# A hand-written order for the first batch: a new order of pieces, other engines for some of them, and exponentials over two PSUM banks

## The chip, the cores and the metric

The kernel runs on one core of a Trainium2 chip. The metric is the time of one execution in device microseconds (us), the median of several runs. The profile is one further execution, taken apart by engine: PE (TensorE, matmuls and transposes), ACT (ScalarE), DVE (VectorE), POOL (GpSimd), SP (SyncE, which here only starts DMAs).

## The reference

Attention over heads with normed queries and keys, then an MLP with a residual, for 8 batches of 448 tokens, 12 heads of 64:

```python
q_n, k_n = rmsnorm(q, g_q), rmsnorm(k, g_k)               # over the last axis, 64
scores = q_n @ k_n.T / 8 ; attn = softmax(scores)
x = (attn @ v), heads side by side                        # 8 x 448 x 768
xn = (x - mean) / sqrt(var + 1e-6) * g_ln
out = x + relu(xn @ w_ch1) @ w_ch2                        # 768 -> 3072 -> 768
```

## The kernel before

Heads are worked in pairs: pair p is heads 2p and 2p+1 of a batch, so pairs 0 to 5 are batch 0 and 6 to 11 batch 1. Pairs come in units that are loaded and normed together: units 0 and 1 are pairs 0 and 1, unit 2 is pairs 2 and 3, unit 3 pairs 4 and 5, and from unit 4 on each unit is two pairs. The matmuls take fp16 operands; a key is split into a high and a low fp16 part.

From batch 1's MLP on, loops set the order of the work. All that comes before that, batch 0 and the attention of batch 1 up to pair 12, is written out by hand as one list of short names, `ORDER`. `first_attention` walks the list and calls one closure for each name. Every engine takes its instructions strictly in the order of that list, and waits where an operand or a buffer isn't ready. `ENGINE` says for some names which engine does them (A is ACT, V is DVE, P is POOL); the rest have a usual engine.

The names that the text uses:

- keys of unit u in batch 0: `a` square, `d` sum, `h` root (`h0` to `h3`, `hq`, `hr`; each is two short ACT instructions), `n` scale, `j` high part, `k` low part; then for pair p `Kp` is the transposition on PE and `Cp` the copy out of PSUM. Later units add `b`, `c`, `e`, `g`, `i`, `l`, `m` (queries, root, weights) and `Qp`, `Dp`.
- queries of batch 0, by phase and first pair (`q0.2`): `qa` square, `qt` sum, `qG` times the weight, `ql` scale, `qm` doubling, `Q` transposition, `QC` copy out of PSUM. `sp1`, `spm`, `sp2` make the product of the two norm weights (a small PE matmul in between).
- `Sph.p.k`, `Eph.p.k`, `Vph.p`: scores, exponential and values of phase ph (a third of the query rows) of pair p in batch 0. A phase 0 or 1 score takes two banks, k = 0 (512 columns) and k = 1 (384). `O`, `T`, `A`, `N`, `X`, `XC`: the attention's output, its layer norm, and the transposition of the normed tokens.
- `Ut.k`: 24 matmuls of the first MLP layer for token tile t and 512 of the 3072 columns of w_ch1, `Rt.k` the relu that empties its bank. `Ht.g.k`, `Jt.g`, `Pt.g`: second layer, residual, store.
- `L5k`: load of unit 5's keys. `W0`, `W1`, `W2`: thirds of w_ch1 (1024 columns each), started by POOL; `U?.0` and `U?.1` need W0, `U?.2` and `U?.3` W1, `U?.4` and `U?.5` W2. `W3.k`, `W4.k`: quarters of the halves of w_ch2. `B0`, `B2`...: a tiny POOL copy that waits for a load, and so holds back the W behind it (`BEHIND` says which load).
- `F12`: 12 filler matmuls, whose result nobody reads.

PSUM has eight banks: one for transpositions (`tr`), two for scores (pool `ps_s`, tile `psS`), two for values (`ps_o`, tiles `oA` and `oB`) and three for the MLP, the query transpositions and a few others (`ps_m`). So a 512-column score sits in one bank, and each exponential reads one bank.

## Time and profile before

| | |
|---|---|
| time, median of 3 runs | 591.55 us (591.08 to 592.36) |
| profiled execution | 591.01 us, of which the span from first to last instruction 589.4 us |
| PE busy | 577.6 us (98%) |
| ACT, DVE, POOL busy | 353.0, 291.7, 189.5 us |
| granted TensorE clock | 1.00 throughout |
| end of the listed part (last `H`) | about 111 us after the start |

A busy PE is one with a matmul in flight; the ends of matmuls are modelled. The DMA share is the mean busy share of 16 DMA engines, where more than 1.00 means that transfers overlap on an engine. A row of the timeline is: start, length, engine, line, operation, tiles, shapes, count, and in brackets the idle time just before with what ended it.

### The profile page before, as it was taken

Reading aid. Unit: us, or ns where it says so; the run is one execution under the profiler, and the core shown is the slowest. Engines: PE = TensorE matmul, PEld = TensorE weight load, DVE = VectorE, ACT = ScalarE, POOL = GpSimd, SP = SyncE. Lnnn points to the kernel's source line nnn. Section 1 sums busy time; section 2 is a strip of 40 time slices with the busy share of each in tenths; the row PEclk is TensorE's granted clock in tenths of the full one; section 3 lists DMA queues with packets and bytes.
Section 4 is the critical chain, followed back from the end, with each engine's and each line's share of the span. In section 5 each row is a group of like instructions: output and inputs, shape, how many; then the busy total and the mean of one; then the engine's idle time right before and its main releaser. Section 6 shows DMA issues by size and latency. Waiting matters only on the chain.

```text
span 589.4 us, 12424 instructions
## 1 busy us (share of the span) xinstructions
PE 577.6 (98%) x4971; PEld 360.4 (61%) x4971; DVE 291.7 (49%) x636; ACT 353.0 (60%) x666; POOL 189.5 (32%) x258
## 2 busy tenths in 40 slices
PE   5899999999999999999999999999999999999997
PEld 5799976545666666545566666655566566654565
DVE  6999688345545456624446256815266222540011
ACT  5999773488752997178842797358844477124300
POOL 4648261065350665044350465342502000000000
PEclk9999999999999999999999999999999999999999
DMA  8999998573594987843779596844823220030011
GB/s 266 226 246 219 228 220 213 115 192 89 114 181 125 132 161 115 191 131 66 124 133 158 99 140 140 174 133 92 155 59 88 69 63 1 33 103 1 1 53 57
DMA packets 130321, 75.25 MB, mean 128 GB/s; under 512 B 96564, under 2 KB 120452, under 8 KB 130260
## 3 DMA queue, kind: packets, MB, share of 16 engines
q1 hardware_dynamic: 113712, 44.94, 37.3%
q0 software_dynamic: 16224, 29.27, 23.7%
q8 instruction: 40, 0.66, 0.5%
q10 hardware_dynamic: 324, 0.21, 0.1%
q14 instruction: 21, 0.17, 0.1%
HBM read 52.30 MB, written 11.01 MB: 107 GB/s over the span
## 4 chain that ended last, share of the span: by engine, by line
PE 95%; SPq 2%; DVE 1%; DMA 1%; ACT 0%; issue 0%
PE psC L1090 37%; PE psH L1056 33%; PE psS L408 8%; PE oA L477 5%; PE psU L749 4%; PE oB L479 2%; PE psS L426 2%; PE psS L693 1%; SPq L167 1%; SPq L175 1%; PE oA L725 1%; DMA qkv<-in_q_dram 1%; PE tr L345 1%; PE tr L362 0%; ACT E L704 0%; DVE khl L573 0%
## 5 line engine op out<-in xcount | busy, mean ns | idle before, releaser
L1090 PE MATMUL psC<-w,hT 128*128 128x384 f16 (+1 forms) x1368 | 235.6, 323 | 0.0
L1056 PE MATMUL psH<-xnT,w 128*128 128x512 f16 (+1 forms) x1008 | 217.3, 356 | 0.0
L440 ACT ACTIVATE E<-psS,rr_all 128x448 f16<-128x448 f32 x264 | 164.6, 636 | 58.3 <-PE psS L408 57.6
L1090 PEld LDWEIGHTS <-hT 128*128 128x128 f16 x1368 | 128.2, 98 | 75.9 <-issue 0.4
L1058 ACT ACTIVATE hT<-psH 128x512 f16<-128x512 f32 (+1 forms) x168 | 93.7, 558 | 112.3 <-PE psH L1056 110.8
L1056 PEld LDWEIGHTS <-w 128*128 128x128 f16 x1008 | 91.1, 98 | 77.0 <-issue 2.1
L408 PE MATMUL psS<-qU,kU 128*128 128x448 f16 x252 | 86.3, 352 | 0.0
L477 PEld LDWEIGHTS <-E 128*128 128x128 f16 x792 | 53.6, 98 | 34.4 <-issue 2.1
L1097 DVE SCALAR_TENSOR_TENSOR x<-psC,rs_all,x 128x384 f32<-128x384 f32 x48 | 29.0, 616 | 75.6 <-PE psC L1090 75.1
L274 POOL TENSOR_TENSOR qkv<-qkv,gprod 128x896 f32<-128x896 f32 x19 | 39.5, 2079 | 76.9 <-ACT khl L116 62.4
L477 PE MATMUL oA<-v,E 128*128 128x65 f16 x756 | 57.8, 193 | 0.1
L490 DVE RECIPROCAL rec_all<-oA 128x6 f32<-128x6 f32 x42 | 8.2, 195 | 88.6 <-PE oA L477 88.2
L167 POOL DMA_DIRECT2D qkv<-in_k_dram x14 | 11.1, 796 | 118.3 <-ACT E L440 53.4
L266 DVE TENSOR_REDUCE ssq<-khl 128x14 f32<-128x896 f32 x21 | 22.7, 1083 | 53.3 <-ACT khl L116 53.2
L479 PE MATMUL oB<-v,E 128*128 128x65 f16 x252 | 45.0, 193 | 0.1
L408 PEld LDWEIGHTS <-kU 128*128 128x128 f16 x252 | 24.3, 98 | 15.3
L266 DVE TENSOR_REDUCE ssq<-qn 128x14 f32<-128x896 f32 x21 | 22.8, 1084 | 21.1 <-ACT qn L116 21.1
L91 DVE SCALAR_TENSOR_TENSOR qn<-qkv,rr_all 128x256 f16<-128x256 f32 (+2 forms) x71 | 25.3, 416 | 15.1 <-ACT rr_all L270 15.1
L749 PE MATMUL psU<-xnT,w 128*128 128x128 f16 x432 | 27.0, 219 | 0.0
L749 PEld LDWEIGHTS <-w 128*128 128x128 f16 x432 | 25.2, 98 | 1.5 <-issue 0.4
L479 PEld LDWEIGHTS <-E 128*128 128x128 f16 x264 | 25.4, 96 | 0.3 <-DVE xl L497 0.2
L492 DVE TENSOR_TENSOR x<-oA,rec_all 128x384 f32<-128x384 f32 x42 | 23.4, 558 | 1.3
(161 smaller groups left out, 602.5 us busy)
## 6 DMA issues: line engine op xcount, KB each, us to landing
out_dram<-x SPq DMA_DIRECT2D x20, 384.0 KB, 2.6
qkv<-in_v_dram POOLq DMA_DIRECT2D x15, 384.0 KB, 6.6
qkv<-in_k_dram POOLq DMA_DIRECT2D x14, 384.0 KB, 4.0
qkv<-in_q_dram POOLq DMA_DIRECT2D x14, 384.0 KB, 4.9
w<-in_moe_w_ch_dram POOLq DMA_DIRECT2D x3, 1536.0 KB, 13.2
...
```

The costliest lines, as they stand in the source:

```text
L91: nc.vector.scalar_tensor_tensor(out=out, in0=x, scalar=8.0, in1=r.unsqueeze(2).broadcast_to([x.shape[0], g, D]), op0=ALU.mult, op1=ALU.mult)
L266: nc.vector.tensor_reduce(out=c["ssq"][:, n], in_=c["sq", n], axis=AX.X, op=ALU.add)
L274: _on(nc, f"i{u}", "P").tensor_tensor(out=self.loads[u][1], in0=self.loads[u][1], in1=sh.gprod.unsqueeze(1).broadcast_to([128, g, D]), op= ...
L408: self.nc.tensor.matmul(ps[:, 0:S], c["main"][:, ts(i, 128)], c["q"][:, ts(i // 3, S)], start=True, stop=True)
L440: self.nc.scalar.activation(out=o, in_=c.pop(("ps", i))[:, 0:S], func=AFT.Exp, scale=self.units[u][3][:, g:g + 1], bias=EXP_BIAS)
L477: nc.tensor.matmul(oA[:, t, cs], E[:, ts(t, 128)], rhs, start=(i == 0 and t == 0), stop=(i == 6 and t == 2))
L479: nc.tensor.matmul(oB[:, cs], E[:, 320:448], rhs, start=(i == 0), stop=(i == 6))
L749: nc.tensor.matmul(ps[:, ts(f, 128)], sh.w1[:, dc, ts(4 * k + f, 128)], self.xnT[:, dc, ts(t, 128)], start=(f == 0 and dc == 0), stop=(f = ...
L1056: nc.tensor.matmul(ps[:, 0:N], sh.w1[:, dc, ts(f, 128)], xnT[:, dc, 0:N], start=(dc == 0), stop=(dc == NDC - 1))
L1058: nc.scalar.activation(out=hT[:, f, 0:N], in_=ps[:, 0:N], func=AFT.Relu)
L1090: nc.tensor.matmul(self.psC[:, 0:g[1]], self.hT[:, f, ts(t, 128)], sh.w2[:, h, f, c:c + g[1]], start=(f == 0), stop=(f == NFF - 1))
L1097: self.nc.vector.scalar_tensor_tensor(out=x, in0=self.sums.pop((b, t, g[0]))[:, 0:g[1]], scalar=self.rs[:, b, t:t + 1], in1=x, op0=ALU.mul ...
```

## The change

1. `ORDER` is a new list. It holds the same pieces, but for twelve exponentials that are merged into twelve others, two new pieces `I9` and `I10` (a one-column POOL memset that claims the buffer of unit 9 or 10 ahead of its load), and the fillers: 91 matmuls before, 143 after.
2. `ENGINE` gives other engines to some 45 pieces. Of those ahead of the first `U`: `n0 n1 k0 k1 ql0.2 qa2.4 qG2.0` go to POOL; `j0 j3 qG0.0 qG0.2 QC0.0 qm2.0 qm2.4` to DVE; `C0 C3 QC1.0 QC2.2 QC2.4` to ACT. Later: seven of the relus from ACT to DVE, and squares, casts and subtractions of units 4 to 8 mostly to POOL.
3. The two halves of a phase 0 or 1 score lie in one tile of two banks, read by one exponential of 896 columns. There are two such tiles (pools `ps_w0`, `ps_w2`). After the twelfth they are closed and their four banks become single banks; two of them go to scores, two join bank 4 for the MLP. Until then bank 4 alone serves all that `ps_m` served.
4. The keys' fp16 parts of batch 0 get room of their own in `hT`, and the key transpositions alternate between two banks (`tr` and the bank of `oB`).
5. `W0` waits for the last values of batch 0 (`BEHIND[0]`) instead of the keys of unit 4; `W1` no longer follows at once.

```diff
-BEHIND = {0: (4, 1), 2: (5, 2), 3: (6, 2), 4: (7, 2)}
+BEHIND = {0: (0, 2), 2: (5, 1), 3: (6, 1), 4: (7, 1)}
 ORDER = """
-F12 a0 a1 d0 h0 sp1 spm qa0.0 n0 sp2 qt0.0 d1 qG0.0 j0 h1 k0 L4k G ql0.0 n1 F14 K0 Q0.0 j1 L4q a2
+a0 d0 h0 a1 L4k F12 n0 qa0.0 j0 F8 sp1 qt0.0 F14 d1 k0 F10 spm F5 h1 sp2 K0 qG0.0 a2 n1 F4 F2 j1
+ql0.0 F4 F9 d2 k1 G Q0.0 L4q QC0.0 C0 qa0.2 qa1.0 F39 qt0.2 F5 h2 K1 qG0.2 ql0.2 B0 n2 F6 W0 a3
...
-        self.ps_s = pool("ps_s", 2, space=PSUM)
-        self.ps_m = pool("ps_m", 3, space=PSUM)
+        self.room = {4: pool("ps_4", 1, space=PSUM)}
+        for at in (0, 2):
+            self.whole[at] = tc.tile_pool(name=f"ps_w{at}", bufs=1, space=PSUM, side=SIDE[at])
+            self.room[at] = self.whole[at].__enter__()
+        self.n_wide, self.wide, self.idle, self.free, self.read, self.free_s = 0, [2, 0], [4], [], {}, False
+        self.tr2 = self.ps_o.tile([128, 1024], FP16, tag="oB", name="tr2")
+    def two_banks(self):
+        at = self.wide.pop(0)
+        self.n_wide += 1
+        if self.n_wide == 2 * NPAIR:
+            for x in self.wide:
+                self.wide_read(x)
+        return at, self.room[at].tile([128, 1024], FP32, tag=f"wide{at}", name="psW")
+    def wide_read(self, at):
+        if self.n_wide < 2 * NPAIR:
+            self.wide.append(at)
+            return
+        self.whole[at].__exit__(None, None, None)
+        for y in (at, at + 1):
+            self.room[y] = self.ctx.enter_context(
+                self.tc.tile_pool(name=f"ps_{y}", bufs=1, space=PSUM, side=SIDE[at]))
+        if not self.free_s:
+            self.free_s = True
+            self.free += [at + 1, at]
+        else:
+            self.idle += [at, at + 1]
+    def score_psum(self):
+        at = self.free.pop(0)
...
+    def mlp_psum(self):
+        self.at = self.idle.pop(0)
+        return self.bank(self.at)
...
         def power(ph, p, k):
-            width = 192 if ph == 2 else 128
+            if ph < 2:
+                nc.scalar.activation(out=E[ph, p], in_=psS[ph, p][:, 0:896], func=AFT.Exp,
+                                     scale=0.125, bias=EXP_BIAS)
+                self.wide_read(psS["at", ph, p])
+                return
...
+                ops[f"C{p}"] = lambda p=p: self.moved(f"C{p}", kT[p], banks[p % 2][:, 0:960])
...
-                warm["ps"] = self.ps_o.tile([128, 3, 130], FP32, tag="oB", name="psW")
+                warm["ps"] = self.ps_o.tile([128, 3, 130], FP32, tag="oA", name="psW")
...
+            ops[f"I{u}"] = lambda u=u: nc.gpsimd.memset(self.load_tile(u)[1][:, 0, 0:1], 0.0)
```

Three places of the new order follow, each as instructions of one engine. DVE from the sum of unit 0's key squares (`d0`) on, before; `hT` is the buffer that holds the keys, `khl` their fp16 parts, `L566` is `n0` and `n1`, `L573` is `k0` and `k1`:

```order
L555 TENSOR_REDUCE ssq<-khl 128x7
L795 TENSOR_TENSOR gprod<-w_62 1x64
L566 TENSOR_TENSOR hT<-hT,rr_all 128x448
L800 COPY gprod<-psG 128x64
L555 TENSOR_REDUCE ssq<-qn 128x4
L555 TENSOR_REDUCE ssq<-khl 128x7
L573 TENSOR_TENSOR khl<-hT,khl 128x7x64
L612 TENSOR_TENSOR qn<-qkv,rr_all 128x4x64
L566 TENSOR_TENSOR hT<-hT,rr_all 128x448
L785 COPY kT<-tr 128x960
L573 TENSOR_TENSOR khl<-hT,khl 128x7x64
```

The same stretch of DVE after (`five` is a single bank):

```order
L627 TENSOR_REDUCE ssq<-hT 128x7
L117 CAST hT<-hT 128x7x64
L889 TENSOR_TENSOR gprod<-w_62 1x64
L627 TENSOR_REDUCE ssq<-qn 128x4
L627 TENSOR_REDUCE ssq<-hT 128x7
L894 COPY gprod<-five 128x64
L679 TENSOR_TENSOR qkv<-qkv,gprod 128x4x64
L686 TENSOR_TENSOR qn<-qkv,rr_all 128x4x64
L627 TENSOR_REDUCE ssq<-hT 128x14
L879 COPY qU_100<-five 128x512
```

The scaling, the low parts and the copy of pair 0's keys have left DVE; a cast (`j0`), a weighting (`qG0.0`) and the copy of the first queries (`QC0.0`) have come, and the copy of `gprod`, which waits for the small PE matmul, stands behind both sums.

ACT at the first exponentials, before; each reads one bank `psS`:

```order
L783 COPY qU_106<-psQ 128x1024
L704 ACTIVATE E<-psS 128x512
L704 ACTIVATE E<-psS 128x384
L601 ACTIVATE qn<-qkv 128x4x128
L601 ACTIVATE qn<-qkv 128x4x64
L704 ACTIVATE E<-psS 128x512
L601 ACTIVATE qn<-qkv 128x2x128
L601 ACTIVATE qn<-qkv 128x2x64
L704 ACTIVATE E<-psS 128x384
L704 ACTIVATE E<-psS 128x512
```

And after, where `psW` is a tile of two banks:

```order
L599 ACTIVATE rt<-ssq 128x26
L600 ACTIVATE rr_all<-rt 128x26
L782 ACTIVATE E<-psW 128x896 x2
L877 COPY kT<-tr_126 128x960
L123 ACTIVATE khl<-qkv 128x4x128
L123 ACTIVATE khl<-qkv 128x4x64
L877 COPY qU_101<-five 128x768
L782 ACTIVATE E<-psW 128x896 x2
L599 ACTIVATE rt<-ssq 128x12
```

Two exponentials have become one, the second root `h3` stands ahead of all of them, and two copies that DVE made are between them.

POOL around the loads of w_ch1 (`L963`), before: W0 and W1 stand together, behind the poke that waits for unit 4's keys, and ahead of the values' casts (`L661`, `L666`):

```order
L605 TENSOR_TENSOR qkv<-qkv,gprod 128x12x64
L838 COPY poke<-w_62 128x2
L963 DMA w_68<-in_moe_w_ch_dram 128x6x1024 x2
L661 CAST v_108<-qkv 128x12x64 x2
L666 CAST vl<-qkv 64x2x64 x4
L661 CAST v_108<-qkv 128x12x64
L666 CAST vl<-qkv 64x2x64 x2
L887 TENSOR_SCALAR gln<-gln 128x768
```

After, from W0 to W1 (W2 follows three instructions later):

```order
L1060 DMA w_68<-in_moe_w_ch_dram 128x6x1024
L679 TENSOR_TENSOR qkv<-qkv,gprod 128x12x64
L742 CAST vl<-qkv 64x2x64
L737 CAST v_102<-qkv 128x12x64 x2
L742 CAST vl<-qkv 64x2x64 x3
L125 TENSOR_TENSOR khl<-qkv 128x2x128
L125 TENSOR_TENSOR khl<-qkv 128x2x64
L742 CAST vl<-qkv 64x2x64 x2
L737 CAST v_102<-qkv 128x12x64
L679 TENSOR_TENSOR qkv<-qkv,gprod 128x8x64
L679 TENSOR_TENSOR qkv<-qkv,gprod 128x256
L1060 DMA w_68<-in_moe_w_ch_dram 128x6x1024
```

W0 is now ahead of the query weighting, and W1 behind all the values' casts.

200 lines of the change are left out of this document (125 added, 75 removed).

## The prediction

> **What bounds the kernel now.** I read the page first, then the engines by stage, then PE's timeline. The engines' busy times and the chain that ended last:
>
> ```profile
> PE 577.6 (98%) x4971; PEld 360.4 (61%) x4971; DVE 291.7 (49%) x636; ACT 353.0 (60%) x666; POOL 189.5 (32%) x258
> PE 95%; SPq 2%; DVE 1%; DMA 1%; ACT 0%; issue 0%
> ```
>
> PE sets the end. The change keeps every matmul but the fillers, so it can only win where PE waits, or lose by new waits. By stages of 10 us (busy us of each engine, clock, DMA share, GB/s):
>
> ```profile
> 10.00:20.00 10.00, 8.69 (x130) 7.37 (x127) 9.94 (x13) 9.23 (x17) 3.84 (x5) 1.00 1.04 289
> 20.00:30.00 10.00, 9.36 (x166) 7.94 (x163) 9.93 (x19) 9.37 (x24) 9.61 (x14) 1.00 1.08 224
> 30.00:40.00 10.00, 9.94 (x182) 9.59 (x180) 9.86 (x20) 9.55 (x23) 5.87 (x6) 1.00 1.12 220
> 40.00:50.00 10.00, 10.00 (x190) 9.59 (x187) 8.90 (x18) 8.74 (x17) 6.55 (x9) 1.00 1.02 256
> 50.00:60.00 10.00, 10.00 (x172) 9.17 (x170) 9.74 (x17) 9.77 (x19) 6.87 (x10) 1.00 1.18 223
> ```
>
> From 10 to 30 us DVE is full (9.94 and 9.93 of 10), ACT nearly so, and PE waits; from 30 us on PE is full. DMA is full throughout. PE's timeline at the start, at its last idle row, and at the first `U`:
>
> ```profile
> 3.75 1.46 PE L879 MATMUL psW<-id 128*128 128x128 f16 x12 [3.75 <-POOL id masks.py:199]
> 9.31 0.29 PE L342 MATMUL tr<-id,khl 128*128 128x128 f16 x1 [1.50 <-DVE khl L573]
> 13.93 2.34 PE L879 MATMUL psW<-id 128*128 128x128 f16 x39
> 27.98 0.65 PE L693 MATMUL psS<-qU,kT 128*128 128x128 f16 x6 [0.22 <-ACT E L704]
> 34.76 1.50 PE L749 MATMUL psU<-xnT,w 128*128 128x128 f16 x24
> ```
>
> After 27.98 no wait is left, and from the first `U` (34.76) MLP blocks fill every gap. In both lists the PE pieces ahead of the first `U` are the same (one third of a score is exchanged for another), so the arrival of the first `U`, called T here, measures the start: 34.76 before. What follows is T's shift, then whether PE still runs without waits behind it.
>
> **DVE up to T.** Prices per instruction (mean ns after the count's busy us):
>
> ```profile
> L566 DVE TENSOR_TENSOR hT<-hT,rr_all 128x448 f32<-128x448 f32 x2 | 1.2, 622 | 1.6 <-ACT rr_all L540 1.6
> L573 DVE TENSOR_TENSOR khl<-hT,khl 128x448 f16<-128x448 f32 x2 | 1.2, 622 | 0.0
> L785 DVE COPY kT<-tr 128x960 f16<-128x960 f16 x3 | 2.0, 655 | 0.0
> L785 DVE COPY qU<-psQ 128x768 f16<-128x768 f16 x5 | 2.8, 552 | 0.0
> L605 DVE TENSOR_TENSOR qkv<-qkv,gprod 128x512 f32<-128x512 f32 x1 | 0.7, 683 | 0.0
> L605 DVE TENSOR_TENSOR qkv<-qkv,gprod 128x256 f32<-128x256 f32 x1 | 0.5, 517 | 0.0
> ```
>
> Gone: `n0 n1 k0 k1` 4 x 0.622 = 2.49; `ql0.2`, 512 wide, 0.68; `C0 C3` 2 x 0.655 = 1.31; `QC1.0 QC2.2` 2 x 0.552 = 1.10; `qG2.0` 0.683 + 0.517 = 1.20; together 6.8. Come: `qG0.0` 0.52 and `qG0.2` 0.68. `j0`, `j3`, `QC0.0`, `qm2.0` and `qm2.4` have no row on DVE: at most the two-operand price of their widths or that of the copy (0.62 + 1.24 + 0.55 + 0.55 + 0.55 = 3.5), at least about 1.5, if a copy between fp16 tiles (0.39 for 896, quoted below) sets the scale. I take 2.0, nearer to the copies, because four of the five have one operand of fp16 or PSUM. Net: 6.8 - 1.2 - 2.0 = 3.6 us less on the engine that is full; 2.1 to 4.1 by the ends.
>
> Not all of it shortens T, since the chain now hops between engines. `n0` and `k0` go to POOL, which has room: it waited 4.3 and 4.6 us in this stage.
>
> ```profile
> POOL poke L838 <- DMA w<-in_k_dram: 4.6, 1, 4.6
> POOL qkv L605 <- DVE gprod L800: 4.3, 1, 4.3
> L605 POOL TENSOR_TENSOR qkv<-qkv,gprod 128x512 f32<-128x512 f32 x1 | 1.3, 1268 | 0.9 <-ACT qn L601 0.9
> L274 POOL TENSOR_TENSOR qkv<-qkv,gprod 128x896 f32<-128x896 f32 x3 | 6.2, 2080 | 0.1
> ```
>
> At 448 of 512 each POOL instruction takes about 1.1, half a microsecond longer than on DVE; but `h0` no longer stands behind `a1`, whose data came late, which gives about a microsecond back. So `K0` comes at about 8.5 to 9.6 against 9.31. POOL's own sum up to T grows by about 4.5 (`n0 n1 k0 k1`) + 1.3 (`ql0.2`) + 1.2 (`qa2.4`) + 2.0 (`qG2.0`), less 3.3 for what it gives away: 5.7, inside its waits.
>
> New waits on DVE: the `gprod` copy now stands behind a PE matmul that has 44 fillers ahead of it. The first twelve took 1.46, 0.12 each, so 44 end at 3.75 + 5.4 = 9.1 if PE stays so slow, at about 7.5 if it speeds up to the 0.06 of the row at 13.93. DVE reaches the copy at about 8.3, so it waits 0 to 1.4; I take 0.7, and everything queued on DVE behind it waits too, `ql0.0` and `d2` first. `n3` waits for the root `h3`, which stands on ACT behind the 1024-wide copy `QC0.2`: 0.6 of idle, 0 to 1. Together 1.3. The 52 added fillers cost nothing else, because PE waits for the keys' chain there; without that cover they are 52 x 0.06 = 3.1.
>
> ACT's sum up to T hardly moves by the exchanged pieces. The exponentials:
>
> ```profile
> L704 ACT ACTIVATE E<-psS 128x512 f16<-128x512 f32 x16 | 9.5, 597 | 0.7 <-PE psS L693 0.2
> L704 ACT ACTIVATE E<-psS 128x384 f16<-128x384 f32 x15 | 7.4, 490 | 0.4 <-PE psS L697 0.3
> L783 ACT COPY kT<-tr 128x960 f16<-128x960 f16 x1 | 0.9, 942 | 0.0
> ```
>
> Two took 1.09; one of 896 takes 0.92 if each 128 columns cost 0.107 as between the rows, 0.94 by the 960-wide copy, and 1.09 if crossing a bank costs something. Twelve times that is 0 to 2.0 less. I leave 0 in the sum: DVE, not ACT, carries the layer norm ahead of T. One bank instead of three for the query transpositions makes each `Q` wait for the copy before it; those stand a copy's length apart in the list, so 0, at most one copy, 0.94.
>
> **POOL and DVE at once.** These two can block each other here. Counts, then one DVE copy and the POOL instruction beside it:
>
> ```profile
> L319 DVE COPY qn<-qn x19: 382/394/1749, 40.5 to 467.0; 128x896 f16<-128x896 f16 x19
> 68.22 1.75 DVE L319 COPY qn<-qn 128x896 f16<-128x896 f16 x1
> 67.64 2.08 POOL L274 TENSOR_TENSOR qkv<-qkv,gprod 128x896 f32<-128x896 f32 x1
> ```
>
> The copy that usually takes 0.39 took 1.75, and ended just after the POOL instruction (69.97 against 69.72). The change puts 9 us more work on POOL ahead of T and gives DVE four such copies or casts (`j0`, `j3`, `qm2.0`, `qm2.4`). `j0` is safe, POOL waits for it. The other three can lose up to 1.36 each, 0 to 4.1; I take 1.0, since POOL's instructions there are mostly short casts. The Trainium skill, SBUF — State Buffer, section Who interferes with whom, speaks against the change: a DVE copy in a two-port mode takes a port pair shared with GpSimd for a whole instruction and the other blocks, and a DVE instruction with two SBUF inputs contends with GpSimd's reads. The 1.75 row agrees; by that rule alone every one of these pairs would be a candidate, and the gain here would be gone (the second rival).
>
> T: 3.6 - 1.3 - 1.0 = 1.3 earlier, 33.5.
>
> **Weights behind T.** The new list calls `U1.3`, the first block on W1, and `U1.4`, the first on W2, earlier. PE's rows before `U1.4` at its old place, 58.94, give the prices of the blocks:
>
> ```profile
> 55.37 0.22 PE L342 MATMUL tr<-id,khl 128*128 128x128 f16 x1
> 55.76 1.50 PE L749 MATMUL psU<-xnT,w 128*128 128x128 f16 x24
> 57.10 0.54 PE L408 MATMUL psS<-qU,kU 128*128 128x448 f16 x2
> 57.48 1.50 PE L749 MATMUL psU<-xnT,w 128*128 128x128 f16 x24
> 58.82 0.26 PE L477 MATMUL oA<-v,E 128*128 128x65 f16 x3
> 58.94 1.50 PE L749 MATMUL psU<-xnT,w 128*128 128x128 f16 x24
> ```
>
> A `U` takes 1.34 from start to start, a key transposition 0.39, a score 0.19, a value block 0.12. Between T and `U1.4` lie 24.2 us before. The new list has one `U`, six scores, seven value blocks and one transposition less there: 1.34 + 1.2 + 0.9 + 0.4 = 3.8, so `U1.4` is due at T + 20.4 = 53.9. `U1.3` has three `U`s, ten first-batch scores (0.24 each by their seven or eight short matmuls), three value blocks and two transpositions of 0.35 ahead: T + 8.6 = 42.1. Issues on POOL and landings of W0, then of W0 and W1 (median of two, so W1 took 20.8), then of W2:
>
> ```profile
> 19.95 1.71 POOL L963 DMA_DIRECT2D w<-in_moe_w_ch_dram  x2 [0.27 <-issue]
> w<-in_moe_w_ch_dram POOLq DMA_DIRECT2D x1, 1536.0 KB, 12.5
> w<-in_moe_w_ch_dram POOLq DMA_DIRECT2D x2, 1536.0 KB, 16.7
> 43.51 0.91 POOL L963 DMA_DIRECT2D w<-in_moe_w_ch_dram  x1 [0.27 <-issue]
> w<-in_moe_w_ch_dram POOLq DMA_DIRECT2D x1, 1536.0 KB, 13.2
> ```
>
> W0 landed at 32.5, W1 at 41.6 (9.1 after it), W2 at 56.7. After, W0 is issued at about 15, when batch 0's values are in, and W1 (about 25) and W2 (about 30) are issued before the one ahead has landed. Back to back they need 12.5 + 9.1 + 13.2 = 34.8, so W1 lands at 36.6 and W2 at 49.8, if DMA carries no more beside them than before; the loads that before went between 15 and 20 us at 289 GB/s now go beside W0, some 1.2 MB or 5 us at 220 GB/s: 41.8 and 55.0 at the latest by this. The middle, 39 and 52.4, is ahead of 42.1 and 53.9: cost 0, at most 1.1 at `U1.4`.
>
> Past that the list spreads work so that ACT and DVE get less (seven relus leave ACT, three low parts leave DVE) and POOL more. In 40 to 60 PE was full beside an ACT at 9.77 and a DVE at 9.74; less on both, and POOL at 6.87 with room, cost 0. What hides them is the two score banks and MLP blocks; gone, the longest POOL step, 2.08, is what PE would wait.
>
> **Sum.** 3.6 (DVE) - 1.3 (new waits) - 1.0 (blocked copies) - 0 (exponentials, banks) - 0 (weights) = 1.3 us. The profiled execution took 591.01 with a span of 589.4; it becomes 589.7. The median is 591.55, 0.54 above it: 590.2. A measurement of this kernel tells about 0.2%, 1.2 us, from no change.
>
> **Rivals.** (1) The forecast, faster by 0.6 to 2.0: DVE's 9.94 of 10 speaks for it; against it, that the gain is a difference of three terms. (2) The blocked copies eat it: with two long POOL instructions in the way (2 x 1.36) or blocked two-operand instructions, the third term is 2.3 and the time is 591.5. For it the 1.75 row, against it that 18 of 19 such copies weren't blocked. (3) Slower: W2 lands no earlier than before, 56.7, because the loads of units 4, 5 and 6 all have to go in that time in either order and DMA is full (1.02 to 1.18). Then `U1.4` waits 56.7 - 53.9 = 2.8 and the time is 590.2 + 2.8 = 593.0. It decides from a landing of 55.2 on, where 1.3 is used up. The Trainium skill, DMA: Bandwidth & Descriptors, section Issuing engines are not separate DMA queues, says that DMAs from different engines interleave on the same sixteen; the share above 1 agrees, and it makes this rival a matter of bytes, not of issue times. Against it: DMA dipped when W2's issue was held back to 43.5, 1.9 us behind W1's landing. (4) More: no blocked copy, warm fillers (0.6 of waits) and 3.6 from DVE make T 31.8, and W2 at 49.8 is in time for 52.2: 591.55 - 3.0 = 588.5. For it ACT's 0 to 2.0, against it that ACT then carries the exponentials alone.
>
> **Chances.** (1) 0.48, (2) 0.15, (3) 0.22, (4) 0.15. Faster by over 0.2%: two thirds of (1) and all of (4), 0.47. Within: the rest of (1), 0.12 of (2) and a little of (3), 0.30. Slower: 0.23. The range 588.4 to 593.1 takes in (4) and (3) up to their middles; (1) alone is 589.5 to 591.0.
>
> **What would show it.** Right: the first `U` block at 32.8 to 34.2, DVE less than full in 10 to 30 us, exponentials of 896 at 0.90 to 0.95, PE without an idle row after it, W1 and W2 landed before the first `U` on them. Wrong: an idle PE row in front of a `U` block named with a DMA of w_ch1 (rival 3); a DVE cast or copy over 1 us beside a POOL instruction (rival 2); PE idle after T for another reason, which I priced at nothing.

## The result: slower, 606.37 us against 591.95

The changed kernel took 606.37 us (median of 4 runs, 604.09 to 607.14), the kernel before 591.95 beside it: a ratio of 1.0238 with a 95% interval of 1.0206 to 1.0269. The forecast was 590.2, in a range of 588.4 to 593.1. The profiled executions took 606.48 and 591.01, with spans of 604.8 and 589.4; their difference, 15.5 us, is what is looked for below. An execution over 1.5% above the fastest of its kernel (one each of `a_warm_fill` and `a_warm_apart` below) is left out of a ratio, but not of a median.

From the page of the kernel after: the engines' busy times, the chain that ended last, and the granted clock in 40 slices of 15 us.

```profile
PE 584.4 (97%) x5023; PEld 366.2 (61%) x5023; DVE 297.0 (49%) x635; ACT 344.5 (57%) x641; POOL 215.9 (36%) x275
PE 87%; SPq 4%; DMA 4%; DVE 3%; issue 1%; ACT 0%; DVEq 0%; ACTq 0%
PEclk9779999998999999999999999999999999999999
```

PE is busy 6.8 us longer, although only 52 fillers were added, and it carries 87% of the chain instead of 95%. The clock, 1.00 in all slices of the kernel before, falls in the second and third slice and once more near 145 us. (What lies ahead of the clock's first record, at 13.7 us before and at 7.0 after, is counted as 1.00, but PE runs at half speed there: up to 13.7 us before, its fillers follow each other at 0.107 us, and from there on at 0.056.) By stages of 10 us (columns as in the prediction):

```profile
10.00:20.00 10.00, 6.78 (x125) 6.15 (x123) 10.00 (x10) 8.02 (x13) 8.78 (x9) 1.00 1.11 292
20.00:30.00 10.00, 8.87 (x127) 8.03 (x125) 8.33 (x13) 6.06 (x10) 9.72 (x13) 0.66 1.09 245
30.00:40.00 10.00, 6.84 (x96) 6.27 (x94) 9.10 (x13) 5.66 (x9) 4.85 (x5) 0.71 1.12 227
```

From 10 to 20 us DVE is busy all the time with 10 instructions, where it did 13 before in 9.94; one of them alone takes 3.87 (below). From 20 to 40 us PE has the clock at 0.66 and 0.71. POOL went from 3.84 to 8.78 in the first stage. PE's timeline, its idle rows and the first `U` (`L842`):

```profile
19.47 0.23 PE L398 MATMUL tr<-id,hT 128*128 128x128 f16 x1 [3.20 <-DVE hT L647]
22.05 0.85 PE L709 MATMUL five<-id,qn 128*64 128x128 f16 x12 [1.06 <-DVE qn L686]
35.16 0.82 PE L712 MATMUL five<-id,khl 128*128 128x128 f16 x6 [2.59 <-DVE khl L692]
39.57 0.80 PE L712 MATMUL five<-id,khl 128*128 128x128 f16 x6 [0.57 <-ACT E L782]
42.91 1.50 PE L842 MATMUL five<-xnT,w 128*128 128x128 f16 x24
52.10 0.22 PE L415 MATMUL tr<-id,qn 128*128 128x128 f16 x1 [0.92 <-DVE gmax L946]
122.11 6.64 PE L1154 MATMUL five<-xnT,w 128*128 128x512 f16 x30 [1.52 <-DMA xnT<-xn]
143.58 0.35 PE L537 MATMUL oA<-v,E 128*128 128x65 f16 x3 [2.50 <-DVE x L552]
```

The rows are `K3` (19.47), `Q1.0` (22.05), `Q2.0` (35.16), `Q2.2`, a query transposition of unit 4, the first layer of batch 1's MLP, and a value block behind the list. To see what each is worth I put both PE timelines side by side at equal useful work: each matmul counts with the time that its shape takes at the full clock in the kernel before, from its start to the next start, and the fillers are left out. The kernel after stands

| useful work done, us | 2 | 4 | 6 | 10 | 12 | 14 to 22 | 24 to 80 | 90 to 105 | from 110 on |
|---|---|---|---|---|---|---|---|---|---|
| later than before by, us | -1.9 | 2.5 | 3.5 | 2.9 | 6.8 | 8.0 to 8.3 | 9.1 to 9.3 | 11.2 | 15.5 |

So the start costs 8.1, the row at 52 another 1.1, the one at 122 2.0, the one at 143 4.3: all of the 15.5. The first 2 us of work did come early, as forecast; then two stalls turn the gain over. Each stall of the start is more than its idle time: in 1-us windows after `K3`, after `Q2.0` and after the row at 143 the clock is 0.50 with PE busy throughout.

```profile
24.00:25.00 1.00, 1.00 (x12) 1.00 (x11) 1.00 (x2) 0.24 (x1) 0.94 (x3) 0.50 1.10 225
38.00:39.00 1.00, 1.00 (x13) 0.84 (x11) 1.00 (x3) 0.62 (x2) 0.00 (x0) 0.50 1.10 225
145.00:146.00 1.00, 1.00 (x4) 0.43 (x3) 0.00 (x0) 0.00 (x0) 0.00 (x0) 0.50 1.22 145
```

By the clock's records in the trace it is at half from 20.6 to 27.4 us, from 34.3 to 41.1 and from 143.5 to 146.9: for 6.8, 6.8 and 3.4 us.

Now what PE waited for. DVE's timeline, the three longest rows named in the waits or just behind them (`k2`, `n3`, `qm2.0`), and POOL's beside them:

```profile
15.54 3.87 DVE L647 TENSOR_TENSOR hT<-hT 128x896 f16<-128x896 f32 x1
19.33 1.71 DVE L640 TENSOR_TENSOR hT<-hT,rr_all 128x896 f32<-128x896 f32 x1
31.33 3.77 DVE L692 COPY khl<-khl 128x768 f16<-128x768 f16 x1
```

```profile
15.65 1.82 POOL L679 TENSOR_TENSOR qkv<-qkv,gprod 128x768 f32<-128x768 f32 x1
17.40 0.30 POOL L742 CAST vl<-qkv 64x128 f16<-64x128 f32 x1
17.63 2.46 POOL L737 CAST v<-qkv 128x768 f16<-128x768 f32 x2
...
31.03 1.26 POOL L679 TENSOR_TENSOR qkv<-qkv,gprod 128x256 f32<-128x256 f32 x2
32.25 0.91 POOL L1060 DMA_DIRECT2D w<-in_moe_w_ch_dram  x1
33.19 1.69 POOL L125 TENSOR_TENSOR qn<-w 128x896 f32<-128x896 f32 x1
```

The same `k2` before, with POOL idle beside it:

```profile
17.63 1.08 DVE L573 TENSOR_TENSOR khl<-hT,khl 128x896 f16<-128x896 f32 x1
```

`k2` did not move to another engine and does not do anything else; it takes 3.87 instead of 1.08 because it has POOL's weighting of the queries and two casts beside it. POOL is held in turn: the two value casts at 17.63 take 2.46 together, where two took 1.60 before. `qm2.0` takes 3.77 until POOL is through with two weightings, the issue of W2 and `c4`. POOL has no pause from 12.86 to 34.88 us.

The row at 52 is of the same kind. DVE's scaling and doubling of unit 4's queries take 1.57 and 0.90 just ahead of it, while POOL makes the low part `k4` (which the change gave to it) and casts values; before, with POOL idle beside them, they took 1.08 and 0.38.

The rows at 122 and 143 are another matter. DVE's row ahead of the wait at 143, and SP's queue before that, first of the kernel after, then the stores of the kernel before:

```profile
142.96 0.56 DVE L552 TENSOR_TENSOR x<-oA,rec_all 128x384 f32<-128x384 f32 x1 [4.67 <-DMA out_dram<-x]
...
130.92 1.30 SPq L231 DMA_DIRECT2D qkv<-in_k_dram  x2
132.32 0.54 SPq L1205 DMA_DIRECT2D out_dram<-x  x1
...
136.15 1.57 SPq L1205 DMA_DIRECT2D out_dram<-x  x3
```

```profile
119.34 2.02 SPq L1106 DMA_DIRECT2D out_dram<-x  x4
```

DVE waits for the buffer `x` until batch 0's stores have left it, and these now stand behind and between unit 10's loads (`L231`, `L223`) at the end of the list, 13 to 16 us later than before. Ahead of the row at 122, the transpositions of the normed tokens on SP end at 118.63, and the first layer of batch 1's MLP waits 1.52 for the last.

### The profile page after: what moved, and what is told of

The parts are those of the page before. It is cut to its first block, busy times and chain, and to the rows that moved or that the text cites. A ratio compares the mean times of both kernels' runs of the same rounds, so it can differ in the third digit from the quotient of the medians.

```text
span 604.8 us, 12509 instructions
## 1 busy us (share of the span) xinstructions
PE 584.4 (97%) x5023; PEld 366.2 (61%) x5023; DVE 297.0 (49%) x635; ACT 344.5 (57%) x641; POOL 215.9 (36%) x275
## 4 chain that ended last, share of the span: by engine, by line
PE 87%; SPq 4%; DMA 4%; DVE 3%; issue 1%; ACT 0%; DVEq 0%; ACTq 0%
PE five L1189 34%; PE five L1154 30%; PE five L463 5%; PE oA L537 5%; PE five L842 4%; PE psS L463 2%; DMA w<-in_v_dram 2%; PE oB L539 2%; DMA qkv<-in_v_dram 1%; SPq L231 1%; PE five L481 1%; SPq L223 1%; DMA out_dram<-x 1%; DVE khl L692 1%; SPq L364 1%; SPq L367 1%
## 5 line engine op out<-in xcount | busy, mean ns | idle before, releaser
L1189 PE MATMUL five<-w,hT 128*128 128x384 f16 (+1 forms) x1368 | 235.8, 323 | 0.1
L1154 PE MATMUL five<-xnT,w 128*128 128x512 f16 (+1 forms) x1008 | 218.6, 358 | 1.5 <-DMA xnT<-xn 1.5
L1156 ACT ACTIVATE hT<-five 128x512 f16<-128x512 f32 (+1 forms) x168 | 93.5, 557 | 116.5 <-PE five L1154 115.2
L496 ACT ACTIVATE E<-five,rr_all 128x448 f16<-128x448 f32 x193 | 120.5, 635 | 53.3 <-PE five L463 51.7
L537 PEld LDWEIGHTS <-E 128*128 128x128 f16 x792 | 54.0, 98 | 38.0 <-DVE x L552 3.4
L330 POOL TENSOR_TENSOR qkv<-qkv,gprod 128x896 f32<-128x896 f32 x20 | 41.6, 2080 | 68.4 <-ACT khl L123 53.9
L1195 DVE SCALAR_TENSOR_TENSOR x<-five,rs_all,x 128x384 f32<-128x384 f32 x48 | 29.0, 616 | 74.6 <-PE five L1189 74.1
L463 PE MATMUL five<-qU,kU 128*128 128x448 f16 x181 | 62.5, 353 | 0.0
L223 POOL DMA_DIRECT2D qkv<-in_k_dram x14 | 11.2, 802 | 118.6 <-ACT E L496 53.4
L496 ACT ACTIVATE E<-psS,rr_all 128x448 f16<-128x448 f32 x71 | 44.9, 632 | 9.1 <-PE psS L463 9.1
L322 DVE TENSOR_REDUCE ssq<-qn 128x14 f32<-128x896 f32 x21 | 22.8, 1084 | 20.6 <-ACT qn L123 20.6
L842 PE MATMUL five<-xnT,w 128*128 128x128 f16 x432 | 26.9, 219 | 0.0
L842 PEld LDWEIGHTS <-w 128*128 128x128 f16 x432 | 25.0, 98 | 1.2 <-issue 0.4
```

The source lines that it names most:

```text
L322: nc.vector.tensor_reduce(out=c["ssq"][:, n], in_=c["sq", n], axis=AX.X, op=ALU.add)
L330: _on(nc, f"i{u}", "P").tensor_tensor(out=self.loads[u][1], in0=self.loads[u][1], in1=sh.gprod.unsqueeze(1).broadcast_to([128, g, D]), op= ...
L463: self.nc.tensor.matmul(ps[:, 0:S], c["main"][:, ts(i, 128)], c["q"][:, ts(i // 3, S)], start=True, stop=True)
L496: self.nc.scalar.activation(out=o, in_=ps[:, 0:S], func=AFT.Exp, scale=self.units[u][3][:, g:g + 1], bias=EXP_BIAS)
L537: nc.tensor.matmul(oA[:, t, cs], E[:, ts(t, 128)], rhs, start=(first and t == 0), stop=(last and t == 2))
L842: nc.tensor.matmul(ps[:, ts(f, 128)], sh.w1[:, dc, ts(4 * k + f, 128)], self.xnT[:, dc, ts(t, 128)], start=(f == 0 and dc == 0), stop=(f = ...
```

## The experiments

The theory: POOL's unbroken work holds DVE instructions that read or copy in SBUF; PE then stands idle long enough for the clock to halve; and behind the first `U` the queue of SP makes two more waits. The rivals: the list's order alone, or the engines' table alone, is to blame; the clock is the whole loss; or it is any work on POOL, whatever it does, that costs. Each run was timed beside the kernel before (591.7 to 592.5 in all of them). A name with `a_` starts from the kernel after, one with `b_` from the kernel before.

**What a single trace can tell.** Three of the runs below (`a_stores_first`, `a_tail`, `a_tail2`) change nothing ahead of 100 us. In their traces, as in that of the kernel after, `k2` takes 3.87 and `K3` waits 3.20 to 3.33. The second stall isn't so steady: 2.59 in the kernel after and 2.78 in `a_stores_first`, both ahead of `Q2.0`, 3.00 in `a_tail` ahead of `Q2.4`, and next to nothing in `a_tail2`. Their rows, one of each run in this order:

```profile
36.33 0.82 PE L711 MATMUL five<-id,khl 128*128 128x128 f16 x6 [2.78 <-DVE khl L691]
```

```profile
40.87 0.51 PE L711 MATMUL five<-id,khl 128*128 128x128 f16 x6 [3.00 <-DVE khl L691]
```

```profile
39.38 0.51 PE L711 MATMUL five<-id,khl 128*128 128x128 f16 x6 [0.29 <-DVE khl L691]
```

With the same start, the first `U` comes at 42.91, 43.10, 41.44 and 39.94, and at 20 us of useful work the four are 8.0, 8.2, 6.6 and 5.1 late. So the hold of `k2` is always there, the second hold depends on how DVE and POOL happen to meet, and 3 us at the first `U` of one trace do not show what an edit does. Some traces also are of executions well above their median: `a_hold_pool` 611.87 (606.95), `a_hold_and_double` 607.12 (603.21), `a_apart_tail` 608.82 (603.82), `b_engines_after` 616.54 (611.62), `a_pool_relief` 601.86 (598.34).

**Does POOL hold DVE, and with what?** `b_busy_copy` and `b_busy_set` put work on POOL that nobody needs into the kernel before, just ahead of `B0`: in the first ten casts, which read SBUF, in the second thirteen memsets, which only write.

```diff
+        spare = self.kU[1][:, 0:384]
+        ops["Z0"] = lambda: [nc.gpsimd.tensor_copy(out=spare, in_=<384 of rec_all>) for _ in range(10)]   # b_busy_copy
+        ops["Z0"] = lambda: [nc.gpsimd.memset(spare, 0.0) for _ in range(13)]                             # b_busy_set
-E0.0.1 h2 qt1.0 B0 W0
+E0.0.1 h2 qt1.0 Z0 B0 W0
```

> The kernel before with ten POOL copies that nobody reads (384 fp32 to fp16 each, about 4.5 us together, source and target otherwise idle) ahead of B0, in the stretch from 14.9 to 19.5 us in which POOL waits for a load while DVE scales the keys and makes their low parts. Theory L (DVE instructions with two operands in SBUF wait as long as POOL reads SBUF without a pause): n2, ql0.2 or n3 there takes 2 to 5 us instead of about 1, PE's waits in 15 to 25 us grow by 2.5 to 4.5, the time rises to 595 to 598. Rival (POOL's work beside DVE is harmless, the stalls come from the order): 591.5 to 592.5.

> The same with thirteen POOL memsets (384 fp16 each) in place of the ten copies: POOL is as busy, but only writes. Theory L as the trace suggests it (a shared read path): DVE is not held, 591.5 to 592.5. If POOL's writes hold DVE as well: as the copies, over 594.

`b_busy_copy`: 596.48, ratio 1.0062 (1.0039 to 1.0084). `b_busy_set`: 592.46, ratio 0.9994 (0.9983 to 1.0006). Timelines, POOL's filling and the same `k2` of DVE beside it, casts first, memsets second:

```profile
14.92 9.56 POOL L841 CAST kU<-rec_all 128x384 f16<-128x384 f32 x10
18.54 1.39 DVE L573 TENSOR_TENSOR khl<-hT,khl 128x896 f16<-128x896 f32 x1
```

```profile
15.70 6.12 POOL L841 MEMSET kU<- 128x384 f16 x13
18.45 1.08 DVE L573 TENSOR_TENSOR khl<-hT,khl 128x896 f16<-128x896 f32 x1
```

Memsets leave DVE at 1.08, casts make it 1.39, and the casts take 0.96 each, longer than a value cast of twice the width in the same run (0.83): reading is what collides. But here DVE lost 0.3 an instruction, not 2.8; the two took turns, and the expected hold of 2 to 5 us did not come. Only part of the 4.0 us of `b_busy_copy` is the collision, since its W0 and value casts also start later, PE waits 1.14 and 0.99 for those, and the clock is at half for 3.4 us behind.

**The holds taken away one by one.** `a_hold_pool` puts POOL's nine pieces (the weighting `qG1.0`, value casts, `qa2.4`) behind a tiny POOL copy `Z0` that reads the result of `k2`; `a_double_pool` gives the doubling `qm2.0` back to POOL; `a_hold_and_double` does both.

```diff
-qG1.0 ... za0 z0 z2 za3 zb0 ... za2 ... qa2.4 zb2 ... k2          # a_hold_pool
+k2 Z0 qG1.0 za0 z0 z2 za3 zb0 za2 qa2.4 zb2
-qm2.0:V                                                            # a_double_pool
+qm2.0:P
```

> The changed kernel with one engine put back: the doubling copy qm2.0 on POOL instead of DVE. Theory L (a DVE instruction waits while POOL works on without a pause, PE then idles, and after an idle stretch of this length its clock is granted at one half for some 6 us): the 3.77 us copy is gone from DVE, PE's idle row of 2.59 before the last third's query transposition (35.16) falls below 0.8, the clock stays at 1.00 between 34 and 41 us, and the time falls from 606.4 to about 602.0 (2.6 idle and 1.8 of slow matmuls). Rival R (the new order as such is late, whatever engine doubles): the copy takes 0.8 on POOL behind W2's start, the next thing is late instead, and the time stays within 605.4 to 606.4. Rival I (blocking yes, but the clock isn't tied to idleness): 603.8 and a clock still at one half there.

> The changed kernel with POOL held back once: a tiny POOL copy that reads the low part k2 (so POOL waits until DVE has made it) stands ahead of nine POOL pieces (qG1.0, qa2.4 and the casts of the values z0, z2, za0, za2, za3, zb0, zb2), which now follow k2. Nothing is taken off any engine and one wait is added. Theory L: k2 takes about 1.1 instead of 3.87 and the scaling n3 behind it 1.1 instead of 1.71, PE's idle row of 3.20 at 19.47 shrinks below 1, the clock stays at 1.00 from 20 to 28 us, and the time falls to 601 to 603.5. Rival R: POOL gets its work 1 us later and the time rises to 606.5 to 608. Rival I: idle time falls by about 3, the clock does not recover, 603 to 604.

> Both edits together. Theory L: the two stalls are separate, so the gains add: 597 to 600, the first U at 34.5 to 37 instead of 42.9, no clock below 1.00 before 100 us. What is then left over 592 stands in the later idle rows (0.9 at 52, 1.5 at 122, 2.5 at 143.6 with its own stretch of half clock, about 7 together). Rival R: less than 3 us gained, over 603. Rival P (the later idle rows follow from the start being late and vanish with it): 591 to 594.

`a_double_pool`: 604.32, ratio 1.0189 (1.0167 to 1.0211). `a_hold_pool`: 606.95, ratio 1.0244 (1.0225 to 1.0263). Both: 603.21, ratio 1.0194 (1.0172 to 1.0217). PE's `Q2.0` in `a_double_pool`, then DVE's `k2` and `ql1.0` and PE's `Q1.0` in `a_hold_pool`:

```profile
35.05 0.51 PE L712 MATMUL five<-id,khl 128*128 128x128 f16 x6 [1.49 <-POOL khl L692]
```

```profile
16.45 1.09 DVE L646 TENSOR_TENSOR hT<-hT 128x896 f16<-128x896 f32 x1
20.50 2.57 DVE L685 TENSOR_TENSOR qn<-qkv,rr_all 128x768 f16<-128x768 f32 x1
23.12 0.77 PE L708 MATMUL five<-id,qn 128*64 128x128 f16 x12 [4.13 <-DVE qn L685]
```

In `a_double_pool` the wait shrinks from 2.59 to 1.49, the clock stays 1.00 from 30 to 40 us, and some 2 us are won by the medians, though the intervals of the two kernels' ratios just touch and this stall differs from one execution to the next anyhow. In `a_hold_pool` `k2` is back at 1.09, so POOL's pieces were what held it; but now they stand beside `n3` (2.69) and `ql1.0` (2.57), and PE waits 4.13 one step later. `a_hold_and_double` shows the same three (2.70, 2.57 and 4.13), and so the two gains, expected to give 597 to 600, did not add. The hold moves with the work.

`a_apart` tries to have nothing of POOL beside DVE: value casts on ACT, `qG1.0` ahead of `B0`, `ql0.2` back on DVE, `qa2.4` and `c4` on ACT, both doublings on POOL.

```diff
-                nc.gpsimd.tensor_copy(out=<v16, vl>, ...)
+                nc.scalar.copy(out=<v16, vl>, ...)
-ql0.2:P qa2.4:P c4:P qm2.0:V qm2.4:V
+qm2.0:P qm2.4:P
```

> The changed kernel with POOL's reads kept apart from DVE's work ahead of the first U; every piece is still there. The casts of the values (z, za, zb) go to ACT behind C3, QC1.0 and E0.2.0; qG1.0 stands ahead of B0; ql0.2 goes to DVE, qa2.4 and c4 to ACT, qm2.0 and qm2.4 to POOL. The end of the list is untouched. Theory L: k2, n3, ql1.0 and k3 take 1.1 or less, the idle rows of 3.20 and 2.59 go, the clock is 1.00 up to 100 us, the first U comes at 34 to 37 instead of 42.9; with the rows at the end left (6.2 us) the time is 597 to 600.5. Rival R (the new order is late by itself, with more on ACT and DVE now): the first U no earlier than 40, over 603.

605.43, ratio 1.0234 (1.0197 to 1.0271). `k2` takes 1.08 and `n3` 1.09, as they do alone, and the first `U` comes at 39.76. But `K3` still waits 2.45, since `qG0.2` on DVE was held beside the moved `qG1.0` (2.13 instead of 0.67), and ACT, at 9.86 and 9.89 of 10 from 20 to 40 us, becomes what PE waits for (1.48 and 1.55 on exponentials).

**List or table?** `a_engines_before` is the new list with the old `ENGINE`, `b_engines_after` the old list with the new one.

```diff
-ENGINE = <that of the kernel>
+ENGINE = <that of the other kernel>
```

> The changed kernel's list with the engine table of before, so that only the order (and the banks) is changed. Theory O (the order of the list makes the stalls: it puts W0's start, qG1.0 and the casts of the values on POOL just when DVE scales and subtracts the keys): k2 takes over 2.5 us beside POOL's casts as in the changed kernel, the idle row behind it stays, qm2.0 is on POOL and its stall goes, the later idle rows at the end of the list stay: 601 to 606. Theory E (the engine table does it, by putting more work on POOL): k2 at 1.1, no idle row over 1 us before the first U, about 592 to 597.

> The kernel before (list, banks, loads) with the engine table of the changed one. Theory L (what holds DVE is POOL's reads beside it; the table adds 9 us of them ahead of the first U): some DVE instructions of 10 to 30 us get longer by 0.5 to 2 us, 592.5 to 598. Theory E of the prediction (DVE was full and gets 3.6 us less to do): 589 to 591.5.

610.48, ratio 1.0298 (1.0272 to 1.0323), and 611.62, ratio 1.0338 (1.0313 to 1.0363). Each alone is slower than both together. The new list stalls at `K3` with the old engines too (3.77). The new engines stall the old list already at `K0` (3.51), and at 38.27 the same queries' transposition waits 2.80 for DVE. So the loss can't be put down to the list alone or to the table alone: each of them without the other loses more.

**The clock.** `a_warm_fill` puts 53 fillers ahead of `K3` and 17 ahead of `Q1.0`, so that PE is busy while it waits.

```diff
-S0.1.0 zb3 K3 F4 ql1.0 K2 z3 F4 E0.1.0 j3 Q1.0 F4
+S0.1.0 zb3 F53 K3 F4 ql1.0 K2 z3 F4 E0.1.0 j3 F17 Q1.0 F4
```

> The changed kernel with 70 more filler matmuls: 53 (3.2 us) ahead of K3, where PE idles 3.20, and 17 (1.0 us) ahead of Q1.0, where it idles 1.06. The waits themselves stay. Theory L: the clock stays at 1.00 from 20 to 28 us; what is won is only the slow matmuls there, 5.9 us of streaming at half speed less what the waiting engines hide, so 1.5 to 2.5: 604 to 605. Rival I (the clock falls for another reason, at a set time or by load): it falls all the same, and the fillers in the slow stretch cost up to 2 us, 606.4 to 608.5.

606.48, ratio 1.0222 (1.0188 to 1.0256), single runs from 602.55 to 614.26: no gain that stands clear of the noise. Its stage of 20 to 30 us, and DVE's `ql2.4` with POOL's `c4`, `a4` and the next weighting beside it:

```profile
20.00:30.00 10.00, 9.24 (x168) 7.96 (x166) 9.96 (x14) 6.75 (x11) 9.72 (x13) 1.00 1.10 241
```

```profile
36.93 3.97 DVE L685 TENSOR_TENSOR khl<-qkv,rr_all 128x256 f16<-128x256 f32 x2
34.49 1.69 POOL L124 TENSOR_TENSOR qn<-w 128x896 f32<-128x896 f32 x1
36.27 2.28 POOL L124 TENSOR_TENSOR khl<-w 128x896 f32<-128x896 f32 x1
38.63 2.13 POOL L329 TENSOR_TENSOR w<-w,gprod 128x896 f32<-128x896 f32 x1
```

The clock is 1.00 where it was 0.66. From 2.5 to 10 us of useful work this kernel falls 2.9 us behind the kernel before, the kernel after 4.6, and the three others with its start 3.5 to 4.9. So the fillers save 1.7 us against the kernel after (0.6 to 2.0 against the others), and that is about what the first half clock cost. What follows can't be laid to them: `qm2.0` gets through, `ql2.4` is held instead and PE idles 2.99 at `Q2.4`, but so it does in `a_tail`, without fillers. From 110 us of work on, this execution is 13.5 late against 15.5 for the kernel after, and far behind the list it loses 2.4 again:

```profile
365.54 0.35 PE L480 MATMUL psS<-qU,kU 128*64 128x448 f16 x1 [2.03 <-DMA qU<-qn]
```

A wait of this kind, for a transposition of queries by DMA, stands in the traces of `a_pool_relief` (2.34 at 361), `b_engines_after` (2.03 at 374) and `a_apart_tail` (3.31 at 229) too, and in no other. Why it comes in some executions only is open.

**The later rows.** `a_stores_first` only moves unit 10's loads behind the four stores. `a_tail` and `a_tail2` do that and put the transpositions `Y.X` each behind its norm, `a_tail` also `K13 C13` behind the norms; `a_apart_tail` is `a_apart` with the edits of `a_tail2`.

```diff
-x8 L10k S12.2 J0.1 P0.1 J2.0 E12.2 L10v E12.3 E12.4 L10q P2.1 P1.1 P2.0     # all four
+x8 S12.2 J0.1 P0.1 J2.0 E12.2 E12.3 E12.4 P2.1 P1.1 P2.0 L10k L10v L10q
-Y.N0 L9q za8 S12.1 Y.N2 L9v ... Y.X0 Y.N3 ... Y.X3 Y.X2 Y.N1 ... Y.X1         # not a_stores_first
+Y.N0 Y.X0 L9q za8 S12.1 Y.N2 Y.X2 L9v ... Y.N3 Y.X3 ... Y.N1 Y.X1
```

> The changed kernel with the end of its list put in another order: the stores P0.1, P1.1, P2.0, P2.1 ahead of unit 10's loads on SP's queue, each transposition of batch 1's normed tokens (Y.X) right behind its norm, and K13 with C13 behind the norms. The start is untouched. Theory T (these two rows are made by the end of the list: 1.5 of idle on xnT at 122, 2.5 of idle and 3 us of half clock at 143 because a store stands behind loads): the rows shrink to under 0.5 each, the time falls by 4 to 5.5, to 601 to 602.5. Rival P (they follow from the late start): they stay, 606.

> The changed kernel with the two moves at the end of its list that the run before left standing, without the one that made a new wait: stores ahead of unit 10's loads, each Y.X right behind its norm; K13 and C13 stay at their place. Theory T: the idle row at 143 and its half clock go (about 4.1), the one at 122 shrinks from 1.5 to under 1, and no new row comes: 601 to 602.5. Rival P: 604 or more.

> Both: POOL's reads apart at the start, and the end of the list as in the first of this set. Theory L with T: the two gains add, since they lie 70 us apart on an engine that is full between them: 592 to 596; under 591.5 only if the start is then earlier than before's. Rival P: they overlap, over 598.

> The changed kernel with nothing but unit 10's three loads (L10k, L10v, L10q) moved behind the four stores at the end of the list; the transpositions Y.X and unit 9's loads keep their order on SP. Theory T: the stores go out about 4 us earlier, the row of 2.5 us at 143 and the half clock behind it are gone, the row of 1.5 at 122 stays: 601.5 to 603. Rival (another wait takes its place, as in the two runs before that also moved Y.X): over 604.5.

`a_stores_first`: 602.34, ratio 1.0186 (1.0168 to 1.0204), 4.0 us below the kernel after. The row at 143 and its half clock are gone, the one at 122 is still 1.52. `a_tail`: 604.37, ratio 1.0208 (1.0181 to 1.0236); `a_tail2`: 605.66, ratio 1.024 (1.0215 to 1.0265); `a_apart_tail`: 603.82, ratio 1.02 (1.0176 to 1.0225). PE's timeline in `a_tail`, then in `a_tail2`:

```profile
114.92 0.27 PE L414 MATMUL tr<-id,qn 128*128 128x128 f16 x1 [3.40 <-DVE kU L407]
```

```profile
122.46 9.20 PE L1153 MATMUL five<-xnT,w 128*128 128x512 f16 x30 [4.53 <-DMA xnT<-xn]
```

Both lost at one place what the stores gave at the other. In `a_tail` the copy `C13`, moved behind the norms, left the next query transposition waiting (the row at 122 is gone there). In `a_tail2` the transpositions now had unit 9's loads between them on SP, 1.8 us twice, so PE waited 4.5 instead of 1.5 for the last; in `a_apart_tail` it waited 4.1 there. Only the stores were a clean edit.

**Together.** `a_warm_apart` has the fillers, `c4` and `a4` on ACT and both doublings on POOL; `a_warm_apart_stores` adds the stores; `a_pool_relief` further takes `G2` to DVE, `qa2.4` to ACT (behind `qa2.0`) and W2 behind `qm2.0`; `a_pool_relief_dve` is that with the doublings on DVE. `a_relief_hold` takes the last, puts `qG1.0` on DVE, holds the nine value casts behind `ql1.0`, and has 20 and 10 fillers.

```diff
-c4:P a4:P qm2.0:V qm2.4:V                                # a_warm_apart
+qm2.0:P qm2.4:P
-qa2.4:P                                                   # a_pool_relief
+G2:V
-S1.0.0 W2 S1.0.1 ... E1.3.0 qm2.0 S1.2.0
+S1.0.0 S1.0.1 ... E1.3.0 qm2.0 W2 S1.2.0
-qm2.0:P qm2.4:P                                           # a_pool_relief_dve
+qm2.0:V qm2.4:V
+qG1.0:V                                                   # a_relief_hold
-F53 K3 ... ql1.0 ... F17 Q1.0
+F20 K3 ... ql1.0 Z0 z0 za0 zb0 z2 za2 zb2 z3 za3 zb3 ... F10 Q1.0
```

> The changed kernel with the 70 fillers of the earlier run (53 ahead of K3, 17 ahead of Q1.0), qm2.0 and qm2.4 on POOL, and the squares c4 and a4 on ACT. The values' casts and qG1.0 stay on POOL, so k2 is still held. Theory L (held DVE instructions and the half clock behind them are the two parts of the start's loss): the clock stays at 1.00 up to 40 us, no DVE instruction of 28 to 42 us is held for over 1 us, the first U comes at 38 to 39.5 instead of 42.9, with the 3.2 us wait at K3 left in it: 601 to 603. Rival A (with that, ACT or the two score tiles are the next limit ahead of the first U): it comes at 40.5 or later, over 604.

> Both edits of this set. Theory L with T: 597 to 599.5; what is left over 592 is then K3's wait (3.2), the row at 52 (0.9) and the row on xnT (1.5). Rival A: over 600.

> As a_warm_apart_stores, and POOL's unbroken chain ahead of the last third's queries shortened by 5 us: the scaling of gln (G2, 2.18 on POOL) goes to DVE, the squares qa2.4 (1.91) to ACT, and W2's start (0.92) stands behind qm2.0. qm2.0 and qm2.4 are on POOL. Theory C (in the changed kernel POOL has no pause from 13 to 35 us; whatever stands at the end of that chain is late, a held copy on DVE or the copy itself on POOL): Q2.0's idle row of 3.40 shrinks below 0.5 and no half clock follows, the first U comes at 36.5 to 38 instead of 41.8, the time is 596.5 to 598.5. Rival A (ACT's exponentials in two score tiles are the next limit at once): first U at 40 or later, over 600.

> The same with qm2.0 and qm2.4 on DVE, as in the changed kernel. Theory C: POOL pauses earlier, so the copies are held for at most one POOL instruction (under 1.3 instead of 3.77): 596.5 to 599. If it is the engine of the doubling by itself that costs: 600 to 602, with a copy of over 2 us.

> As a_pool_relief_dve, and the last held stretch ahead of K3 taken away: qG1.0 on DVE (about 0.95 more there), the nine casts of the values on POOL behind a tiny copy that reads ql1.0's result, so that POOL rests while DVE makes k2, n3 and ql1.0; fillers 20 and 10 instead of 53 and 17. Theory L (k2 held for 2.8 us and n3 for 0.6 are the largest piece left of the start's loss): k2 and n3 take 1.1 each, K3 starts at 17.7 to 18.5 instead of about 20, the first U comes at 35 to 36 instead of 37.1, the time is 596 to 597.3. Rival A (something else, ACT or the two score tiles, then ends last): the first U stays at 36.8 or later, 598 or more.

| | median, us | ratio to before (95%) | first `U` |
|---|---|---|---|
| `a_warm_apart` | 607.78 | 1.029 (1.0251 to 1.0328) | 40.93 |
| `a_warm_apart_stores` | 601.94 | 1.0173 (1.016 to 1.0186) | 41.42 |
| `a_pool_relief` | 598.34 | 1.0101 (1.0083 to 1.0119) | 37.63 |
| `a_pool_relief_dve` | 598.21 | 1.0104 (1.0084 to 1.0124) | 37.14 |
| `a_relief_hold` | 597.91 | 1.0093 (1.0078 to 1.0108) | 37.55 |

(The runs of `a_warm_apart` spread from 603.74 to 613.56.) PE's `Q2.0` in `a_warm_apart`; then the doubling on DVE, the first `U` and the stage of 30 to 40 us in `a_pool_relief_dve`:

```profile
34.33 0.51 PE L711 MATMUL five<-id,khl 128*128 128x128 f16 x6 [3.40 <-POOL khl L691]
```

```profile
30.23 0.66 DVE L691 COPY khl<-khl 128x768 f16<-128x768 f16 x1
37.14 1.50 PE L841 MATMUL five<-xnT,w 128*128 128x128 f16 x24
30.00:40.00 10.00, 9.18 (x168) 8.75 (x165) 8.58 (x21) 9.92 (x18) 0.72 (x1) 1.00 1.13 233
```

With the doubling on POOL, `Q2.0` waits 3.40: the doubling takes 0.84 there, but stands behind POOL's weightings, `G2` and W2's issue. Once POOL has room (0.72 of 10), the same doubling takes 0.66 on DVE and holds nothing up, and it makes no difference which engine does it (598.34 and 598.21). So neither of the two engines is wrong for the doubling; a POOL without a pause is, by holding DVE or by its own queue. The relief is worth 3.6 us (601.94 to 598.34).

`a_relief_hold` was to win what was left at the start and did not: `k2` is at 1.07 and `n3` at 1.08, but `qG1.0` takes 1.80 on DVE, `K3` waits 1.14 behind it, and the first `U` is no earlier. About 6 us of the loss stay in the best versions. Counted by useful work as above, `a_pool_relief_dve` is 1.7 to 3.0 us late from 4 to 22 us of work, 4.5 to 4.7 from 24 on and 6.6 from 90 on. The first step comes at `K3`: `k2` still takes 3.87 in its trace, and fillers only stand in for the idle PE. The second comes with the wait ahead of unit 4's query transposition, where DVE's scaling of these queries takes 2.29 beside POOL's `k4` and value cast (1.08 before):

```profile
47.54 0.23 PE L414 MATMUL tr<-id,qn 128*128 128x128 f16 x1 [1.50 <-DVE qn L374]
```

The third is the wait for the transpositions of the normed tokens, 1.48 at 117.51. No run takes the second or third away cleanly, so their prices are readings of the trace. No version beat the kernel before.

## Why the prediction was wrong, point by point

- **What bounds the kernel.** Right: PE sets the end, and the change could only lose by new waits. Whether "PE still runs without waits behind it" was the right question, and it was answered by busy shares.
- **DVE's 3.6 us less.** Some of it came: at 2 us of useful work PE was 1.9 early. The first hold used that up; the size of the term cannot be read behind it. Of the new waits (1.3), the copy of `gprod` did not wait at all (8.36, right behind the sum before it), and `n3` stood behind the held `k2`.
- **Blocked copies, 1.0 of 0 to 4.1.** The term that failed. I charged it only to copies and casts that the change gave to DVE, at most 1.36 each by the one 1.75 row. The holds were 2.8 on `k2` and 0.6 on `n3`, two-operand instructions that the change did not touch, and over 3 on `qm2.0` alone, the last not in every execution. The 1.75 row had one POOL instruction beside it; here there were several in a row, and DVE waited for the whole row.
- **POOL's sum, "5.7, inside its waits".** The step behind that. Those waits of 4.3 and 4.6 were not spare room: they were the pauses in which DVE got through. Filled, they left POOL busy from 12.86 to 34.88. An engine at 3.84 of 10 is free to take work only if no one else needs its silence.
- **The clock.** Not priced at all. I took PE's idle time as its cost; in fact two stalls of the start were each followed by 6.8 us at half clock. The first of these cost about 1.7. At the second, 5.4 us are lost from 10 to 13 us of useful work, with 2.59 and 0.57 of idle PE in them; the rest, some 2, goes with the half clock.
- **The second rival** had the right mechanism and the right sign, at 591.5 with a chance of 0.15. Its price was two blocked copies (2 x 1.36 is 2.7, not the 2.3 that it put in); it missed that they lie on PE's path and halve the clock. I weighed it by the 18 of 19 copies that were not blocked, which say nothing about a POOL without pauses. The rule of the Trainium skill quoted there (SBUF — State Buffer, Who interferes with whom) was the right lead, and the trace now bears it out on `k2` and `qm2.0`.
- **Weights (third rival).** Right to cost nothing: no `U` waited for w_ch1. W1 was issued at 27.99 and W2 at 32.25, and they landed at 41.3 and 50.8 (39 and 52.4 were forecast). With the prices quoted, the way from T to `U1.3` adds up to 7.5 and not 8.6, but nothing hung on it.
- **Exponentials.** Right: 12 of 896 columns at 0.915, between 0.90 and 0.95.
- **Past T, "cost 0".** Wrong by 7.4 (1.1, 2.0 and 4.3). I looked at busy shares of DVE, ACT and POOL and never at the queue of SP, though unit 10's loads and batch 0's stores both changed places; `a_stores_first` shows 4.0 of it. The 1.1 at 52 is the failed term again: "three low parts leave DVE" put one of them on POOL beside DVE's work on the same unit.

The exponentials' row, by lines, up to 42 us:

```profile
L782 ACT ACTIVATE E<-psW 128x896 f16<-128x896 f32 x12 | 10.2, 915 | 6.6 <-PE psW L773 3.5 <-PE psW L777 3.1
```
